# Rearranged start of an attention-and-MLP kernel: first chunk on hardware queues, weight folded by blocks, filler matmuls, one transpose moved to PE

## Chip, cores, metric

One core of a Trainium2 chip. The metric is the device time of one execution in microseconds (us), as the median of several; "span" is the time from the first to the last instruction in a trace. The wait that a view gives for PE runs from the modelled end of the matmul before; from start to start about 0.16 us more of PE's time is lost.

## The reference

```python
# q, k, v: (4, 6080, 256) float32; moe_w_in (256, 2048); moe_w_out (2048, 256)
qn = q / (norm(q, axis=1) + 1e-6);  kn = k / (norm(k, axis=1) + 1e-6)   # norms over the 6080 rows
s  = kn.transpose(0, 2, 1) @ qn / tau                # 256 x 256 for each of 4 batches
a  = softmax(s)                                      # last axis
x  = (v @ a).reshape(24320, 256)
h  = relu(x @ w_in)
out = (moe_s * h * h + moe_b) @ w_out
```

## The kernel before

For each batch the kernel sums the 256 x 256 Gram matrix of k and q and the squares for the norms, takes the exponentials, and folds the attention matrix into the first weight (`wa` = a @ w_in), so that v goes straight through `wa`. A fold is two matmuls and an eviction, which copies their result out of PSUM, where the kernel lets matmuls write (for 128x512 of it 0.69 us on ACT, 0.75 on DVE). The main loop is 48 groups of 512 rows of v, in 16 steps each: a step is `mm1` (two matmuls of 512 columns into `h_ps`), a relu on ACT, a square on DVE, and `mm2` of the steps four and five earlier (four matmuls of 256 into `o_ps`). Everything else (Gram matmuls of the next batch, loads, casts) is hung on steps with `at_step`.

```python
        def load(self, c):                       # all chunks: POOL queue, cast fp32 -> fp16 in flight
            at, np_, jc = self.chunks[c]
            ...
            for t, src in ((kc, k), (qc, q)):
                po(nc.gpsimd.dma_start(out=t[:np_, :jc, :], in_=...))
    ...
    for c in range(len(g0.chunks)):
        g0.load(c)
    po(nc.gpsimd.dma_start(out=w_in16, in_=...))            # whole first weight, then v
    load_v(0)
    for h in range(2):
        po(nc.gpsimd.dma_start(out=w_out32[...], in_=...))  # second weight, two halves
    load_v(1); load_v(2)
    ...
    nc.sync.dma_start(out=s_bc, in_=moe_s.to_broadcast((P, 1)))   # 128 reads of 4 bytes
    nc.sync.dma_start(out=b_bc, in_=moe_b.to_broadcast((P, 1)))
    ...
    for f in fin[:3]: f()           # norms, reciprocals, transposes of S
    transpose_v(0)                  # first group of v: on PE
    for f in fin[3:]: f()           # exponentials, sums, all eight folds of 512 columns
    ...
        if g >= 1:                  # every later group of v: transposed by DMA (crossbar)
            at_step(max((g - 2) * FT, 4 * (g - 1)) + 6, lambda g=g: crossbar_v(g))
    ...
    def fold_w(fo, m):              # 2 matmuls, then an eviction: m == 0 on ACT, m == 1 on DVE
    ...
    def rowconst_sum(i, n): ...     # 8 sums on DVE, one a step from step 8
    at_step(8 + len(todo), rowconst_mm)
```

## Time and profile before

| | before |
|---|---|
| time, median of 4 | 769.46 us (769.11 to 769.82) |
| span | 768.4 us |
| PE busy | 734.9 us, 96% |
| first h_ps matmul (start of the main loop) | 48.91 us |
| PE idle, waiting for group 1 (the second; counted from 0) | 5.0 us before 65.99, then half clock to 71.6 |

The lines of the profile are in the prediction below. A window row gives the busy time of PE, PEld (weight loads), DVE, ACT and POOL, then the granted PE clock, the DMA engines' busy share and GB/s written. A timeline row is start, length, engine, source line, operation, and in brackets the idle time before it and what is thought to have ended it.

### The profile page before, as it was taken

To read this page: it belongs to the slowest core of one execution; us is meant where nothing else is said; L and a number is where in the kernel's file an instruction comes from. 1 tells how busy PE (TensorE), PEld (TensorE's weight loads), DVE (VectorE), ACT (ScalarE), POOL (GpSimd) and SP (SyncE) were. 2 spreads that over 40 slices of the span, in tenths; PEclk is the share of its full clock that TensorE was granted. 3 is DMA by queue.
4 is the path that set the end of the run, shared out by engine and by line. 5 is a ranking of instruction groups with operands and counts; after the bars stand their busy time and mean duration, and the time that the engine had idled before them with its cause. 6 is when DMAs were issued, how large, how long until landed. Compare 5 with 4: busy or idle time off the path is not lost.

```text
span 768.4 us, 14012 instructions
## 1 busy us (share of the span) xinstructions
PE 734.9 (96%) x5274; PEld 507.1 (66%) x5274; DVE 479.4 (62%) x1059; ACT 517.7 (67%) x858; POOL 57.3 (7%) x111
## 2 busy tenths in 40 slices
PE   3587999999999999999999999999999999999997
PEld 2444666666667666666667666666667766666666
DVE  3755666766566666667556666676656556565565
ACT  3464777776767777667777667777676666666665
POOL 3411010001000100000001001000000000000000
PEclk9888999999999999999999999999999999999999
DMA  8999945325555274235626565324322333212111
GB/s 155 212 263 173 159 100 112 82 67 115 123 127 132 62 150 108 67 70 109 145 63 121 113 145 114 70 69 80 72 57 77 76 69 90 65 46 83 42 64 42
DMA packets 75988, 78.52 MB, mean 102 GB/s; under 512 B 56320, under 2 KB 56896, under 8 KB 75920
## 3 DMA queue, kind: packets, MB, share of 16 engines
q0 software_dynamic: 15152, 40.51, 28.5%
q1 hardware_dynamic: 60768, 37.12, 18.1%
q8 instruction: 41, 0.67, 0.4%
q14 instruction: 27, 0.22, 0.1%
HBM read 78.91 MB, written 24.90 MB: 135 GB/s over the span
## 4 chain that ended last, share of the span: by engine, by line
PE 90%; DMA 7%; issue 1%; ACT 1%; SPq 0%; POOL 0%; DVE 0%; POOLq 0%
PE o_ps L450 42%; PE h_ps L426 42%; PE s_ps L120 4%; DMA qc<-in_q_dram 4%; DMA v<-in_v_dram 2%; DMA vT<-v 2%; PE wa_ps L237 1%; SPq L283 0%; PE n_ps L185 0%; ACT r L429 0%; ACT eT L214 0%; PE t_ps L208 0%; POOL kc L108 0%; POOL w_out L295 0%; PE rc_ps L347 0%
## 5 line engine op out<-in xcount | busy, mean ns | idle before, releaser
L429 ACT ACTIVATE r<-h_ps 128x512 f16<-128x512 f32 (+1 forms) x768 | 449.9, 593 | 211.9 <-PE h_ps L426 185.0
L436 DVE TENSOR_TENSOR g<-r 128x512 f16<-128x512 f16 (+1 forms) x768 | 320.7, 421 | 254.9 <-ACT r L429 248.0
L426 PE MATMUL h_ps<-vT,wa 128*128 128x512 f16 (+7 forms) x1632 | 454.4, 365 | 5.6 <-DMA vT<-v 5.0
L450 PE MATMUL o_ps<-w_out,g 128*128 128x256 f16 x3040 | 458.3, 273 | 0.0
L450 PEld LDWEIGHTS <-g 128*128 128x128 f16 x3040 | 295.8, 98 | 184.6 <-issue 2.2
L426 PEld LDWEIGHTS <-wa 128*128 128x128 f16 x1632 | 159.6, 98 | 36.2 <-issue 6.3
L120 PE MATMUL s_ps<-qc,kc 128*128 128x256 f16 (+1 forms) x384 | 71.8, 291 | 19.3 <-DMA qc<-in_q_dram 19.2
L458 DVE SCALAR_TENSOR_TENSOR o_sb<-o_ps,s_out,rowconst 128x512 f32<-128x512 f32 x95 | 71.1, 749 | 6.5 <-PE o_ps L450 5.7
L261 POOL DMA_DIRECT2D v<-in_v_dram x48 | 25.8, 537 | 585.2 <-DMA vT<-v 452.7
L143 ACT ACTIVATE sq<-kc 128x1024 f16<-128x1024 f16 (+3 forms) x49 | 50.0, 1031 | 22.0 <-DMA kc<-in_k_dram 18.8
L120 PEld LDWEIGHTS <-kc 128*128 128x128 f16 (+1 forms) x384 | 39.9, 104 | 27.3 <-issue 10.9
L140 DVE TENSOR_TENSOR sq<-qc 128x1024 f16<-128x1024 f16 (+3 forms) x49 | 32.6, 676 | 11.5 <-DMA qc<-in_q_dram 11.5
L156 DVE TENSOR_TENSOR f<-sq 128x1024 f16<-128x1024 f16 (+1 forms) x47 | 31.8, 686 | 0.3
L156 DVE TENSOR_TENSOR f<-f 128x512 f16<-128x512 f16 (+3 forms) x47 | 25.9, 551 | 0.4
L237 PE MATMUL wa_ps<-w_in,eT 128*128 128x512 f16 x64 | 19.8, 415 | 0.0
L242 ACT ACTIVATE wa<-wa_ps,rs 128x512 f16<-128x512 f32 x16 | 11.0, 687 | 9.3 <-PE wa_ps L237 5.2
L108 POOL DMA_DIRECT2D kc<-in_k_dram x26 | 14.2, 546 | 16.0 <-DMA kc<-in_k_dram 8.9
L108 POOL DMA_DIRECT2D qc<-in_q_dram x26 | 14.2, 547 | 9.6 <-DMA qc<-in_q_dram 8.0
L244 DVE TENSOR_SCALAR wa<-wa_ps,rs 128x512 f16<-128x512 f32 x16 | 11.9, 746 | 2.3 <-PE wa_ps L237 2.1
L237 PEld LDWEIGHTS <-eT 128*128 128x128 f16 x64 | 6.6, 105 | 3.7 <-issue 2.5
L214 ACT ACT_TABLE_LOAD x4 | 5.1, 1283 | 0.5 <-DVE rnrm L196 0.5
L343 DVE TENSOR_TENSOR w_out<-w_out 128x512 f32<-128x512 f32 (+1 forms) x8 | 5.2, 651 | 0.0
(37 smaller groups left out, 41.8 us busy)
## 6 DMA issues: line engine op xcount, KB each, us to landing
out_dram<-o_sb SPq DMA_DIRECT2D x47, 512.0 KB, 2.9
v<-in_v_dram POOLq DMA_DIRECT2D x47, 256.0 KB, 3.8
kc<-in_k_dram POOLq DMA_DIRECT2D x20, 512.0 KB, 6.0
qc<-in_q_dram POOLq DMA_DIRECT2D x20, 512.0 KB, 8.8
vT<-v SPq DMA_TRANSPOSE x186, 2.4
w_out<-in_moe_w_out_dram POOLq DMA_DIRECT2D x2, 1024.0 KB, 13.6
kc<-in_k_dram POOLq DMA_DIRECT2D x3, 480.0 KB, 5.7
qc<-in_q_dram POOLq DMA_DIRECT2D x3, 480.0 KB, 8.3
```

Source lines behind the costliest of these rows:

```text
L108: po(nc.gpsimd.dma_start(out=t[:np_, :jc, :], in_=src[self.b, at : at + np_ * jc, :].rearrange("(p j) c -> p j c", j=jc)))
L120: po(nc.tensor.matmul(self.s_ps[:, ch, :], kc[:np_, j, ts(ch, P)], qc[:np_, j, :], start=(c == 0 and j == 0 and ch == 0), stop=(c == len(s ...
L140: po(nc.vector.tensor_mul(st["sq"][:np_, 0, js, :], qc[:np_, js, :], qc[:np_, js, :]))
L143: po(nc.scalar.activation(out=st["sq"][:np_, 1, js, :], in_=kc[:np_, js, :], func=AF.Square))
L156: po(nc.vector.tensor_add(st["f", half][:np_, arrays], src[:np_, arrays, :half, :], src[:np_, arrays, half : 2 * half, :]))
L237: po(nc.tensor.matmul(wa_ps, st["e"][:, j, ts(m, P)], w_in16[:, j, ds(fo * NW, NW)], start=(j == 0), stop=(j == CH - 1)))
L261: po(nc.gpsimd.dma_start(out=v16[:, :nj, :], in_=v_flat[t0 : t0 + nj * P, :].rearrange("(p j) c -> p j c", j=nj)))
L426: po(nc.tensor.matmul(dst, wa[:, ci, ts(m, P)], src, start=(ci == 0), stop=(ci == CH - 1), skip_group_check=True))
L429: po(nc.scalar.activation(out=r16[:, :n], in_=h_ps[:, :n], func=AF.Relu))
L436: po(nc.vector.tensor_mul(g16[:, :n], r16[:, :n], r16[:, :n]))
L450: po(nc.tensor.matmul(o_halves[g, h][:, j % 2, :], g16[:, ts(j, P)], w_out16[:, m, :], start=(m == 0 and j == js[0]), stop=(m == FT - 1 an ...
L458: po(nc.vector.scalar_tensor_tensor(out=o_sb[:, js[0] : js[-1] + 1, :], in0=o_halves.pop((g, h)), scalar=s_out, op0=ALU.mult, in1=rowconst ...
```

## The change

Intent: bring the main loop forward and take the hole behind the first group out. The first chunk comes uncast on the two hardware queues (those of SP and ACT) and is cast on DVE and ACT; POOL makes the identities before its first load; the broadcasts of s and b go behind the third v on the POOL queue; most norm sums stand ahead of the last chunk; a quarter of the first weight comes before v, two 256-wide blocks of it are folded before the loop and the other six folds in it; eight filler matmuls stand in PE's gaps; group 1 of v is transposed on PE at step 12.

```diff
+            direct = self.b == 0 and c == 0
...
+                if direct:
+                    raw = w_out32[:, ds(i * JC, JC), :]
+                    (nc.sync, nc.scalar)[i].dma_start(out=raw, in_=rows)
...
+        def cast(self, c):
...
+                po(nc.vector.tensor_copy(out=kc[:, js, :], in_=w_out32[:, js, :]))
+                po(nc.scalar.copy(out=qc[:, js, :],
+                                  in_=w_out32[:, JC + js.start : JC + js.stop, :]))
...
-    nc.sync.dma_start(out=s_bc, in_=moe_s.to_broadcast((P, 1)))
...
+    load_w_in(0, NW)
+    load_v(0)
+    load_w_in(NW, Dff)
...
+    load_v(2)
+    s_bc = consts.tile([P, 1], FP32)
+    po(nc.gpsimd.dma_start(out=s_bc, in_=moe_s.to_broadcast((P, 1))))
...
+        if c == NCH0 - 1:
+            g0.add_norms()
...
+    fin[0]()
+    fin[1]()
+    keep_busy(6)
+    fin[2]()
     transpose_v(0)
-    for f in fin[3:]:
+    keep_busy(2)
+    for f in fin[3:9]:
...
-    for i in range(1, 8):
-        at_step(i - 1, lambda i=i: cast_w_out(i))
+    for i, f in enumerate(fin[9:]):
+        at_step(i // 2 * 4 + i % 2 + 1, f)
...
+    for i in range(8):
+        at_step(i + 2, lambda i=i: cast_w_out(i))
...
-            at_step(max((g - 2) * FT, 4 * (g - 1)) + 6, lambda g=g: crossbar_v(g))
+            if g == 1:
+                at_step(12, lambda g=g: transpose_v(g))
+            else:
+                at_step((g - 2) * FT + 6, lambda g=g: crossbar_v(g))
```

More of the change, by code (lines that the diff above doesn't have):

```diff
@@ L100, in __init__ @@
             self.tiles = {}
-            self.rows = []
+            self.rows, self.n_ps = [], None
         def load(self, c):
@@ L106, in load @@
             qc = qk_pool.tile([P, JC, C], FP16, tag="qc", name="qc")
-            for t, src in ((kc, k), (qc, q)):
-                po(nc.gpsimd.dma_start(
-                    out=t[:np_, :jc, :],
-                    in_=src[self.b, at : at + np_ * jc, :].rearrange("(p j) c -> p j c", j=jc)))
-            self.tiles[c] = qc, kc
+            direct = self.b == 0 and c == 0
+            for i, (t, src) in enumerate(((kc, k), (qc, q))):
+                rows = src[self.b, at : at + np_ * jc, :].rearrange("(p j) c -> p j c", j=jc)
+                if direct:
+                    raw = w_out32[:, ds(i * JC, JC), :]
+                    (nc.sync, nc.scalar)[i].dma_start(out=raw, in_=rows)
+                else:
+                    po(nc.gpsimd.dma_start(out=t[:np_, :jc, :], in_=rows))
+            self.tiles[c] = qc, kc
+        def cast(self, c):
+            qc, kc = self.tiles[c]
+            for h in range(2):
+                js = slice(h * JC // 2, (h + 1) * JC // 2)
+                po(nc.vector.tensor_copy(out=kc[:, js, :], in_=w_out32[:, js, :]))
+                po(nc.scalar.copy(out=qc[:, js, :],
+                                  in_=w_out32[:, JC + js.start : JC + js.stop, :]))
         def start(self):
@@ L174, in norm_ops, with add_norms @@
             return ops + [fold(2, slice(0, 2), False), fold(1, slice(0, 2), True)]
+        def add_norms(self, last=False):
+            first = self.n_ps is None
+            if first:
+                self.n_ps = ps_h.tile([P, 2, CH], FP32, tag="h_ps", name="n_ps")
+            todo = [(t, np_, j, a, ch) for t, np_, jc in self.rows for j in range(jc)
+                    for a in range(2) for ch in range(CH)]
+            self.rows = []
+            for i, (t, np_, j, a, ch) in enumerate(todo):
+                po(nc.tensor.matmul(self.n_ps[:, a, ch : ch + 1], t[:np_, a, j, ts(ch, P)],
+                                    ones16[:np_, 0:1], start=(first and i == 0),
+                                    stop=(last and i == len(todo) - 1), skip_group_check=True))
         def finish_ops(self):
@@ L180, in norms @@
             def norms():
-                n_ps = ps_h.tile([P, 2, CH], FP32, tag="h_ps", name="n_ps")
-                todo = [(t, np_, j, a, ch) for t, np_, jc in self.rows for j in range(jc)
-                        for a in range(2) for ch in range(CH)]
-                for i, (t, np_, j, a, ch) in enumerate(todo):
-                    po(nc.tensor.matmul(n_ps[:, a, ch : ch + 1], t[:np_, a, j, ts(ch, P)],
-                                        ones16[:np_, 0:1], start=(i == 0),
-                                        stop=(i == len(todo) - 1), skip_group_check=True))
+                self.add_norms(last=True)
                 nrm = sm_pool.tile([P, 2, CH], FP32, tag="nrm", name="nrm")
-                po(nc.scalar.activation(out=nrm, in_=n_ps, func=AF.Sqrt))
+                po(nc.scalar.activation(out=nrm, in_=self.n_ps, func=AF.Sqrt))
                 st["nrm"] = nrm
@@ L229, in sums, with fold_w @@
                 po(nc.vector.reciprocal(out=st["rs"], in_=st["rs"]))
-            NW = 512
-            def fold_w(fo, m):
+            def fold_w(f0, n, m):
                 def f():
@@ L236, in f @@
                     for j in range(CH):
-                        po(nc.tensor.matmul(wa_ps, st["e"][:, j, ts(m, P)],
-                                            w_in16[:, j, ds(fo * NW, NW)],
+                        po(nc.tensor.matmul(wa_ps[:, :n], st["e"][:, j, ts(m, P)],
+                                            w_in16[:, j, ds(f0, n)],
                                             start=(j == 0), stop=(j == CH - 1)))
-                    dst = self.wa[:, m, ds(fo * NW, NW)]
+                    dst = self.wa[:, m, ds(f0, n)]
                     if m == 0:
-                        po(nc.scalar.mul(out=dst, in_=wa_ps, mul=st["rs"][:, m : m + 1]))
+                        po(nc.scalar.mul(out=dst, in_=wa_ps[:, :n], mul=st["rs"][:, m : m + 1]))
                     else:
                         po(nc.vector.tensor_scalar_mul(
-                            out=dst, in0=wa_ps, scalar1=st["rs"][:, m : m + 1]))
+                            out=dst, in0=wa_ps[:, :n], scalar1=st["rs"][:, m : m + 1]))
                 return f
-            return [norms, recip, turn, exps, sums] + [
-                fold_w(fo, m) for fo in range(Dff // NW) for m in range(CH)]
+            widths = ([NW // 2] * 2 if self.b == 0 else [NW]) + [NW] * (Dff // NW - 1)
+            folds, f0 = [], 0
+            for n in widths:
+                folds += [fold_w(f0, n, m) for m in range(CH)]
+                f0 += n
+            return [norms, recip, turn, exps, sums] + folds
     def group(g):
@@ L284, in crossbar_v @@
         vT_tiles[g] = vT
-    grams = {b: Gram(b, chunks_first if b == 0 else chunks_later) for b in range(B)}
-    g0 = grams[0]
-    for c in range(len(g0.chunks)):
-        g0.load(c)
-    po(nc.gpsimd.dma_start(out=w_in16, in_=moe_w_in.rearrange("(co p) f -> p co f", p=P)))
-    load_v(0)
-    w_out_rows = moe_w_out.rearrange("(fo p) d -> p fo d", p=P)
-    for h in range(2):
-        po(nc.gpsimd.dma_start(out=w_out32[:, ts(h, FT // 2), :], in_=w_out_rows[:, ts(h, FT // 2), :]))
-    load_v(1)
-    load_v(2)
     ident16 = consts.tile([P, P], FP16)
@@ L305, with load_w_in @@
     nc.vector.memset(ones32, 1.0)
-    s_bc = consts.tile([P, 1], FP32)
-    nc.sync.dma_start(out=s_bc, in_=moe_s.to_broadcast((P, 1)))
-    b_bc = consts.tile([P, 1], FP32)
-    nc.sync.dma_start(out=b_bc, in_=moe_b.to_broadcast((P, 1)))
-    s_out = consts.tile([P, 1], FP32)
-    nc.vector.tensor_scalar_mul(out=s_out, in0=s_bc, scalar1=1.0 / (LAM * LAM))
+    grams = {b: Gram(b, chunks_first if b == 0 else chunks_later) for b in range(B)}
+    g0 = grams[0]
+    assert FT == 2 * JC
+    g0.load(0)
     warm = consts.tile([P, 1], FP32)
     po(nc.scalar.activation(out=warm, in_=ones32[:, 0:1], func=AF.Sqrt))
+    g0.cast(0)
+    for c in range(1, len(g0.chunks)):
+        g0.load(c)
+    NW = 512
+    w_in_rows = moe_w_in.rearrange("(co p) f -> p co f", p=P)
+    def load_w_in(f0, f1):
+        po(nc.gpsimd.dma_start(out=w_in16[:, :, f0:f1], in_=w_in_rows[:, :, f0:f1]))
+    load_w_in(0, NW)
+    load_v(0)
+    load_w_in(NW, Dff)
+    w_out_rows = moe_w_out.rearrange("(fo p) d -> p fo d", p=P)
+    for h in range(2):
+        po(nc.gpsimd.dma_start(out=w_out32[:, ts(h, FT // 2), :], in_=w_out_rows[:, ts(h, FT // 2), :]))
+    load_v(1)
+    load_v(2)
+    s_bc = consts.tile([P, 1], FP32)
+    po(nc.gpsimd.dma_start(out=s_bc, in_=moe_s.to_broadcast((P, 1))))
+    b_bc = consts.tile([P, 1], FP32)
+    po(nc.gpsimd.dma_start(out=b_bc, in_=moe_b.to_broadcast((P, 1))))
+    s_out = consts.tile([P, 1], FP32)
     g0.start()
-    for c in range(len(g0.chunks)):
+    NCH0 = len(g0.chunks)
+    for c in range(NCH0):
         ops = g0.norm_ops(c)
+        if c == NCH0 - 1:
+            g0.add_norms()
         for j in range(g0.chunks[c][2]):
@@ L322, with keep_busy @@
             f()
+    def keep_busy(n):
+        idle_ps = ps_h.tile([P, TG], FP32, tag="h_ps", name="idle_ps")
+        for _ in range(n):
+            po(nc.tensor.matmul(idle_ps, w_in16[:, 0, :P], w_in16[:, 0, :NW],
+                                start=True, stop=True, skip_group_check=True))
     fin = g0.finish_ops()
-    for f in fin[:3]:
-        f()
+    fin[0]()
+    fin[1]()
+    keep_busy(6)
+    fin[2]()
     transpose_v(0)
-    for f in fin[3:]:
+    keep_busy(2)
+    for f in fin[3:9]:
         f()
@@ L335, in cast_w_out @@
             po(nc.vector.tensor_copy(out=w_out16[:, part, :], in_=w_out32[:, part, :]))
-    cast_w_out(0)
     def rowconst_sum(i, n):
@@ L356 @@
     first_group = [b * N // TG for b in range(B)]
-    for i in range(1, 8):
-        at_step(i - 1, lambda i=i: cast_w_out(i))
+    for i, f in enumerate(fin[9:]):
+        at_step(i // 2 * 4 + i % 2 + 1, f)
+    at_step(14, lambda: po(nc.vector.tensor_scalar_mul(
+        out=s_out, in0=s_bc, scalar1=1.0 / (LAM * LAM))))
+    for i in range(8):
+        at_step(i + 2, lambda i=i: cast_w_out(i))
     todo = [(i, n) for n in (FT * C // 2, FT * C // 4, FT * C // 8, FT * C // 16)
@@ L367 @@
         if g >= 1:
-            at_step(max((g - 2) * FT, 4 * (g - 1)) + 6, lambda g=g: crossbar_v(g))
+            if g == 1:
+                at_step(12, lambda g=g: transpose_v(g))
+            else:
+                at_step((g - 2) * FT + 6, lambda g=g: crossbar_v(g))
     for b in range(1, B):
```

## The prediction

> **What bounds the kernel now.** I read the page first (busy shares, slices), then the windows of the first 72 us, then PE's timeline there, and last the chain, the waits and the DMA issues.
>
> The slices of the page:
>
> ```profile
> span 768.4 us, 14012 instructions
> ...
> PE   3587999999999999999999999999999999999997
> ...
> PEclk9888999999999999999999999999999999999999
> DMA  8999945325555274235626565324322333212111
> ```
>
> A slice is 19.2 us. From the fifth slice on PE is busy without a gap: the main loop is PE-bound to the end, and nothing in the diff makes its matmuls cheaper. All that can be won lies in the first four slices. The windows of that stretch (columns: window, its length, busy time of PE, PEld, DVE, ACT and POOL, PE clock, DMA share, GB/s):
>
> ```profile
> 2.00:4.00 2.00, 0.00 (x0) 0.00 (x0) 0.15 (x1) 0.22 (x2) 2.00 (x5) 1.00 0.58 39
> 4.00:6.00 2.00, 0.00 (x0) 0.00 (x0) 0.00 (x0) 0.00 (x0) 1.62 (x4) 1.00 1.02 158
> 6.00:8.00 2.00, 0.00 (x0) 0.00 (x0) 0.00 (x0) 0.00 (x0) 0.00 (x0) 1.00 0.72 99
> 8.00:10.00 2.00, 0.00 (x0) 0.10 (x1) 0.00 (x0) 1.77 (x2) 0.54 (x1) 1.00 1.04 209
> ...
> 41.00:47.00 6.00, 4.44 (x21) 2.21 (x22) 1.67 (x4) 1.37 (x2) 1.59 (x3) 0.50 1.04 375
> ...
> 61.00:66.00 5.00, 0.01 (x1) 0.04 (x2) 2.46 (x6) 0.20 (x1) 0.00 (x0) 0.85 1.33 156
> 66.00:71.60 5.60, 5.60 (x20) 3.06 (x21) 1.34 (x3) 1.49 (x3) 3.18 (x6) 0.52 0.80 144
> ```
>
> To be seen: the DMA engines do not reach their steady 209 GB/s before 8 us; PE runs its first fold at half clock (0.50 from 41 to 47 us); PE stands from 61 to 66 us and pays for it with half clock (0.52) until 71.6. PE's timeline gives the borders (start, length):
>
> ```profile
> 36.85 0.68 PE L185 MATMUL n_ps<-ones,sq 128*128 128x1 f16 x16 [0.18 <-DVE sq L140]
> 39.10 0.63 PE L208 MATMUL t_ps<-ident,sm_s 128*128 128x128 f32 x4 [1.57 <-DVE sm_s L201]
> 42.56 1.04 PE L272 MATMUL vT_ps<-ident,v 128*128 128x128 f16 x8 [2.83 <-DMA v<-in_v_dram]
> 43.55 5.53 PE L237 MATMUL wa_ps<-w_in,eT 128*128 128x512 f16 x16
> ...
> 65.99 1.01 PE L426 MATMUL h_ps<-vT,wa 128*128 128x512 f16 x2 [4.99 <-DMA vT<-v]
> ```
>
> So the main loop starts behind a wait for v (2.83 us) and 5.53 us of cold fold; the first h_ps matmul comes at 48.91 us in this timeline. The chain of waits names the later stall, the waits what else hangs on it, and the DMA issues how long a transfer queues (last figure: median us from issue to landing):
>
> ```profile
> 52.78 13.07 DMA vT<-v
> ```
>
> ```profile
> POOL v L261 <- DMA vT<-v: 16.5, 1, 16.5
> PE h_ps L426 <- DMA vT<-v: 5.0, 1, 5.0
> ```
>
> ```profile
> w_in<-in_moe_w_in_dram POOLq DMA_DIRECT2D x1, 1024.0 KB, 12.9
> ...
> vT<-v SPq DMA_TRANSPOSE x12, 10.1
> ...
> qc<-in_q_dram POOLq DMA_DIRECT2D x1, 96.0 KB, 9.2
> ```
>
> With the issue times of the POOL timeline (26.22 for the last q, 28.42 for w_in, 30.94 with 11.6 to landing for the first v, 32.19 and 33.39 with 12.9 and 14.3 for w_out), the landings are: last q 35.4, w_in 41.3, v 42.5, w_out 45.1 and 47.7 us. One 512 KB chunk, cast from 1 MB, takes 2.43 us in steady state (the chunks' consumers start at 15.88, 20.85, 25.71, 30.68, two chunks apart).
>
> [...] a DMA share over 1.0 with one queue carrying 88% of it. The hardware queue can therefore win the slow start, not a faster stream. [...] from 52.5 to 62.5 us the crossbar's 256-byte packets go out about one per cast packet, some 50 to 60 per us, and over 300 in half a us once the POOL queue is empty at 63 us. [...] 0.50 after the hole from 37.5 to 42.6, recovery some 5 us after the restart at 66.
>
> **The change part by part.** Times are of the clock of before, shifted as I go.
>
> 1. *First chunk on the hardware queues, s and b moved back.* q and k of the first batch are 12.45 MB of fp32: 12.45/1.05 x 2.43 = 28.8 us of streaming. Landing at 35.4[...] the stream behaves as if begun at 6.0 us. In the trace the first POOL packets start at 2.6 us and then crawl beside the 4-byte packets of the two broadcasts until 7.5 us. The hardware queues gave a first packet at 2.0 us (the broadcast of s), and the broadcasts go behind the third v. A full stream from about 3.7 us gives 2.3 us; the ceiling, from 3.0, is 2.9. The identities now stand ahead of POOL's first load (1.2 us of POOL work), hidden behind 2 MB on the hardware queues. Casts: on DVE two of 128x1024; by the 0.42 us of 128x512 and the slope of such a cast, 0.69 each, 1.4 us. On ACT 1.04 each (as its 1024-wide squares), 2.1 us. DVE has 3.7 us of work per 4.86 us pair of chunks, so it catches up by the fourth pair. Gain 2.3.
>
> 2. *Early norm sums.* They leave 8 matmuls at the end for the 40 of before. But DVE, not PE, is last there: its last square of q ends at 37.1 and n_ps at 37.53. In program order the last chunk's four matmuls now stand behind the sixth chunk's norms, which wait for a DVE square at 36.7. I take a loss of 0.3.
>
> 3. *First quarter of w_in, then v.* The quarter costs 1.2 us of transfer for the 4.9 of the whole, so v lands 3.7 earlier: 42.5 - 3.7 - 2.3 = 36.5, before the transposes of S are done. After n_ps (37.53 - 2.3 + 0.3 = 35.5) come 1.57 of root, reciprocal and product, with six fillers in them (6 x 0.216 = 1.3 warm; 2.6 cold would delay by 1.0), 0.63 of transposes, 0.7 of v's transposes with two fillers (0.43), all beside the Exp table load (1.28) and two exponentials (0.84); then sums (0.3), rs (0.5 with its wait), a 256-wide eviction (0.5). First h_ps at 35.5 + 1.6 + 0.6 + 0.7 + 0.4 + 0.3 + 0.6 + 0.5 = 40.2, say 40.3: 8.6 us before 48.91. This holds gain 1, the wait for v and the cold fold.
>
> 4. *The other six folds go into the loop.* 12 matmuls of 512 at 0.216 = 2.6 us, on PE, which is the bound: given back. Their evictions and the w_out casts fit: in steps 0 to 10 ACT has about 9.7 us of work against PE's 10.4.
>
> 5. *w_out.* Its first half lands at 45.1 - 2.3 = 42.8, cast by 43.3; PE wants it at step 4, 40.3 + 5 x 0.43 + 2 x 0.43 = 43.3. Just met; with ACT's pile-up in steps 0 to 4 I put 0.6 for small stalls.
>
> 6. *Group 1 on PE.* Removes the 5.1 us hole (60.85 to 65.99) and the half clock after it: 5.6 us at 0.52 lose 2.7. Adds eight transposes at about 0.09[...], 0.7.
>
> Sum: 8.6 - 2.6 - 0.6 + 7.8 - 0.7 = 12.5 us. 769.7 - 12.5 = 757.2, 1.6%.
>
> **The rivals.**
> (a) *The stall moves to group 2.* Its crossbar transposes still fight the POOL queue, and POOL no longer stands 16.5 us behind group 1's crossbar: one more v and a k/q pair come in (1.2 + 4.9 us), so the queue empties at 63 - 2.3 + 6.1 = 66.8 and the transposes land near 68. PE needs them at step 32: 40.3 + 15.5 (sixteen steps with folds and transposes) + 13.9 + 2 (Gram matmuls and the row constant) = 71.7. Four us of slack; if it is eaten, 2 to 5 us plus half clock come back: 760 to 764. I give it 12%.
> (b) *The slow start is the memory waking up, not the broadcasts or the software queue.* Then part 1 gives under 1 us: 758.5. [...] against it: the slow stretch is just where the 4-byte packets are.
> (c) *PE stays cold.* If fillers come late for w_in or run cold, about 1 us at the turn and up to 2 in the folds: 760.
> (d) *Everything adds up to more than 2%.* That needs 15.4 us. With the ceiling of part 1 and no stalls I reach 13.7, so something unseen would be needed.
>
> **Range and chances.** 757.0 us; 8 times in 10 between 754.6 and 760.8: below by the ceiling of part 1 and of the stalls, above by one rival of 1 to 4 us. Faster by over 2% (under 754.3): 0.09. Within 2%: 0.90. Slower: 0.01.
>
> **What would show it.** Right: last q's landing near 33 us; DMA at over 350 GB/s (uncast bytes) before 8 us; the first h_ps near 40.3 us; PE clock 1.00 from 36 us on; no idle PE over 1 us after that; no wait for vT; from 90 us on, the same loop, shifted by about 12.5 us. Wrong: a PE wait for vT at group 2, a wait of o_ps for the w_out cast, a clock of 0.5 anywhere after 36 us, or DMA still at 100 to 160 GB/s from 4 to 8 us. If all steps hold and the time is still off by over 3 us, the loop behind 90 us changed, which I don't expect.

From the kernel before: a DMA share of 1.04 at 209 GB/s (8 to 10 us), with 87.8% of the 16 engines' time for the POOL queue from 0 to 90 us; 592 packets of the POOL queue and 576 of the crossbar from 52.5 to 62.5 us; and PE's clock at 0.50 from 40.6 to 47.4 and from 64.5 to 71.3 us. The sum came to 12.5 us, but the 2.3 us of part 1, which stand in its 8.6, start from 6.0 us, and 35.4 - 28.8 is 6.6: the rest is latency. That the first chunk has to be cast on chip is an assumption which no run tests; the 0.09 is the estimate (eight transposes took 0.45 us in the changed kernel).

## The result

The changed kernel took 760.21 us (759.92 to 760.68, 4 runs) against 769.46: a ratio of 0.988 (95% interval 0.9863 to 0.9898), 9.2 us or 1.2% faster, inside 2%. A ratio is the mean time of one kernel's fast runs over that of the other's of the same rounds, so not quite the ratio of the medians quoted. All runs were fast ones (granted clock 0.995 to 0.998). The profiled span fell by 10.3 us.

The page of the changed kernel:

```profile
span 758.1 us, 14053 instructions
...
PE   2689999999999999999999999999999999999998
...
PEclk9999999999999999999999999999999999999999
DMA  9999963337356553326546376233323234312111
```

PE is full from the fourth slice of 19 us on, where it took until the fifth before, and no slice is below 0.9 of full clock. The windows of the changed kernel's start, set against those of before:

```profile
2.00:4.00 2.00, 0.00 (x0) 0.00 (x0) 0.00 (x0) 0.65 (x2) 2.00 (x5) 1.00 0.76 262
4.00:6.00 2.00, 0.00 (x0) 0.00 (x0) 0.00 (x0) 0.00 (x0) 1.99 (x4) 1.00 1.04 418
6.00:8.00 2.00, 0.00 (x0) 0.00 (x0) 0.00 (x0) 0.00 (x0) 0.00 (x0) 1.00 1.01 346
...
41.00:47.00 6.00, 5.01 (x29) 2.54 (x27) 3.78 (x9) 5.08 (x11) 1.20 (x3) 1.00 0.92 257
47.00:61.00 14.00, 11.98 (x82) 7.43 (x80) 11.63 (x26) 8.51 (x15) 1.46 (x3) 1.00 0.96 173
61.00:66.00 5.00, 5.00 (x37) 3.53 (x36) 3.44 (x7) 3.48 (x7) 0.00 (x0) 1.00 0.97 174
```

The stream is at full rate at 4 us (418 GB/s at a DMA share of 1.04, since the first chunk is not halved by a cast; the cast stream of before wrote 209 at the same share), the clock stays at 1.00 from 30 us to the end of the loop (before that it was 0.83 from 20 to 30 us), and the hole from 61 to 66 us is gone. But PE is not full between 41 and 61 us: 16.99 us busy out of 20. PE's timeline shows where:

```profile
39.78 1.04 PE L476 MATMUL h_ps<-vT,wa 128*128 128x512 f16 x4
...
43.75 0.39 PE L476 MATMUL h_ps<-vT,wa 128*128 128x512 f16 x1 [0.99 <-DVE wa L262]
...
48.66 0.39 PE L476 MATMUL h_ps<-vT,wa 128*128 128x512 f16 x1 [0.52 <-DVE wa L262]
...
53.70 0.39 PE L476 MATMUL h_ps<-vT,wa 128*128 128x512 f16 x1 [0.52 <-DVE wa L262]
...
59.41 0.67 PE L390 MATMUL rc_ps<-w_out,ones 128*128 128x256 f32 x2 [0.97 <-PE o_ps L500]
```

The loop starts at 39.78 us, and then stands four times, for 0.99, 0.52, 0.52 and 0.97 us: 3.0 us in all. For the first three the DVE timeline and that of ACT show the queue in front of the folded weight:

```profile
42.60 0.43 DVE L486 TENSOR_TENSOR g<-r 128x512 f16<-128x512 f16 x1 [0.64 <-ACT r L479]
42.95 0.75 DVE L262 TENSOR_SCALAR wa<-wa_ps,rs 128x512 f16<-128x512 f32 x1
...
58.90 0.41 DVE L386 TENSOR_TENSOR w_out<-w_out 128x256 f32<-128x256 f32 x1
```

```profile
41.40 0.69 ACT L260 ACTIVATE wa<-wa_ps,rs 128x512 f16<-128x512 f32 x1
41.97 1.21 ACT L479 ACTIVATE r<-h_ps 128x512 f16<-128x512 f32 x2
```

The eviction of the second half of a fold (42.95) stands in DVE's order behind the square of its step (42.60), that square waits for the relu of its step, and the relu stands on ACT behind the eviction of the first half (41.40). PE needs the columns two steps after the fold and asks too early. DVE does not overtake here: it idles 0.64 us before the square at 42.60 us, though the fold whose eviction stands behind that square ended at 41.52 + 0.59 = 42.11 us. The fourth wait is put down to o_ps, but DVE's last sum for the row constant ends at 58.90 + 0.41 = 59.31, right before rc_ps at 59.41.

### The profile page after: what moved, and what is told of

Read it like the earlier page. It is cut to its first block, busy times and chain, and to the rows that moved or that the text cites. A ratio compares the mean times of both kernels' runs of the same rounds, so it can differ in the third digit from the quotient of the medians.

```text
span 758.1 us, 14053 instructions
## 1 busy us (share of the span) xinstructions
PE 730.5 (96%) x5294; PEld 505.3 (67%) x5294; DVE 480.9 (63%) x1063; ACT 520.1 (69%) x861; POOL 57.8 (8%) x112
## 4 chain that ended last, share of the span: by engine, by line
PE 92%; DMA 3%; DVE 2%; ACT 1%; issue 1%; POOL 1%; DVEq 0%; ACTq 0%; POOLq 0%
PE o_ps L500 43%; PE h_ps L476 42%; PE s_ps L133 4%; DMA qc<-in_q_dram 3%; PE wa_ps L255 1%; ACT r L479 1%; DVE f L169 0%; DVE g L486 0%; ACT eT L234 0%; PE n_ps L198 0%; DVE sq L153 0%; POOL kc L114 0%; DVE wa L262 0%; PE t_ps L228 0%; POOL qc L114 0%
## 5 line engine op out<-in xcount | busy, mean ns | idle before, releaser
L133 PE MATMUL s_ps<-qc,kc 128*128 128x256 f16 (+1 forms) x384 | 69.4, 283 | 18.9 <-ACT qc L123 10.8
L156 ACT ACTIVATE sq<-kc 128x1024 f16<-128x1024 f16 (+3 forms) x49 | 49.9, 1031 | 10.4 <-DMA kc<-in_k_dram 7.4
L255 PE MATMUL wa_ps<-w_in,eT 128*128 128x512 f16 (+1 forms) x68 | 18.9, 366 | 0.0
L260 ACT ACTIVATE wa<-wa_ps,rs 128x512 f16<-128x512 f32 (+1 forms) x17 | 11.2, 662 | 4.6 <-PE wa_ps L255 4.6
L262 DVE TENSOR_SCALAR wa<-wa_ps,rs 128x512 f16<-128x512 f32 (+1 forms) x17 | 12.1, 714 | 0.1
L123 ACT CAST qc<-w_out 128x1024 f16<-128x1024 f32 x2 | 2.0, 1042 | 7.0 <-DMA w_out<-in_q_dram 7.0
```

The lines of the kernel that those rows point to most:

```text
L133: po(nc.tensor.matmul(self.s_ps[:, ch, :], kc[:np_, j, ts(ch, P)], qc[:np_, j, :], start=(c == 0 and j == 0 and ch == 0), stop=(c == len(s ...
L156: po(nc.scalar.activation(out=st["sq"][:np_, 1, js, :], in_=kc[:np_, js, :], func=AF.Square))
L255: po(nc.tensor.matmul(wa_ps[:, :n], st["e"][:, j, ts(m, P)], w_in16[:, j, ds(f0, n)], start=(j == 0), stop=(j == CH - 1)))
```

## The experiments

"Span" is that of all runs of a kernel; the changed kernel's own were 757.9 to 758.2. Different calls ran on different chips or at other times: the kernel before had spans of 767.1 to 768.9 in them, so differences under half a us between calls say little. b_sb_tiny and a_norms_end have two runs, b_sb_late one, whose state is unknown; all others have four, and all of these are fast.

| run | what | median us | ratio to before | spans |
|---|---|---|---|---|
| (changed kernel) | | 760.21 | 0.988 | 757.9 to 758.2 |
| b_g1_pe | before + group 1 on PE | 764.13 | 0.9936 | 762.3 to 763.5 |
| a_g1_crossbar | changed, group 1 on crossbar | 771.29 | 1.0016 | 769.0 to 770.1 |
| a_w_in_whole | changed, weight whole | 763.36 | 0.9924 | 760.8 to 761.8 |
| a_no_fill | changed, no fillers | 761.30 | 0.989 | 759.4 to 760.1 |
| a_sw_chunk | changed, chunk on POOL queue | 761.54 | 0.9899 | 759.0 to 759.4 |
| a_norms_end | changed, norm sums at the end | 759.64 | 0.9876 | 757.8 to 758.0 |
| b_sb_late | before + broadcasts late | 771.53 (1 run) | - | 769.8 |
| b_sb_tiny | before + no broadcasts | 766.86 | 0.997 | 765.1 |
| e_folds_early | changed, folds a step earlier | 758.64 | 0.9854 | 756.7 to 757.1 |
| e_both | and row constant two steps later | 757.66 | 0.984 | 755.4 to 756.1 |
| e_sb_tiny | and no broadcasts | 758.54 | 0.9863 | 756.5 to 756.8 |
| e_order | and weights in order of use | 758.55 | 0.9863 | 756.1 to 756.6 |

All gave correct results.

### The waits in the loop: e_folds_early, e_both

```diff
-        at_step(i // 2 * 4 + i % 2 + 1, f)
+        at_step(i // 2 * 4 + i % 2, f)
```

> The changed kernel with the six folds of the loop each one step earlier. My theory: PE's three waits for a DVE eviction of the folded weight (0.99, 0.52 and 0.52 us in the changed kernel) come from the fold being handed to ACT and DVE, which work in order, only two steps before its columns are used; one step (0.43 to 0.87 us) more takes them away: span 758.1 less 1.8 to 2.0 = 756.1 to 756.3, and no wait of h_ps for wa. Rival: ACT or the w_out casts are short in steps 0 to 6, then the waits only change place and the span stays within 0.4 of 758.1. The wait before rc_ps (0.97) stays under both.

Measured: 756.7 to 757.1, 1.3 us less. The second and third wait are gone, the first shrank from 0.99 to 0.50, a new one of 0.27 for the cast of the second weight stands beside it, and the row constant waits 1.22 instead of 0.97. So the theory holds for its mechanism, and I had its first wait wrong: in steps 0 to 4 ACT and the second weight are short too, as the rival said.

```diff
-    at_step(8 + len(todo), rowconst_mm)
+    at_step(10 + len(todo), rowconst_mm)
```

> The folds one step earlier and the matmul of the row constant two steps later. My theory: the hole of 0.97 us before rc_ps is a wait for DVE's last row-constant sum, which ends at 59.3 us, and two steps (1.7 us) later it is done: all four holes gone, 758.1 less 3.0 = 755.1, in time about 757.2. Rival: the hole is a wait for a free PSUM buffer or the sums only slip further back, then no better than the folds alone (756.2).

Measured: 755.4 to 756.1, 2.3 us under the changed kernel by the means (755.8 and 758.1), not 3.0. PE's waits in e_both (total, times, longest) after the loop's start:

```profile
PE h_ps L476 <- DVE wa L262: 0.4, 1, 0.4
PE o_ps L500 <- DVE w_out L380: 0.3, 1, 0.3
```

The wait at rc_ps is gone, so it was DVE's sums; in e_folds_early, too, the last of them ends at 57.94 and rc_ps starts at 58.03. Behind it a Gram matmul now waits 0.47 us for the first q chunk of the second batch, which the hole had covered. This version, with two numbers changed, beats both kernels: 757.66 us, ratio 0.984.

### Group 1: a_g1_crossbar, b_g1_pe

```diff
-            if g == 1:
-                at_step(12, lambda g=g: transpose_v(g))
-            else:
-                at_step((g - 2) * FT + 6, lambda g=g: crossbar_v(g))
+            at_step(max((g - 2) * FT, 4 * (g - 1)) + 6, lambda g=g: crossbar_v(g))
```

> The changed kernel with the second group of v turned by the crossbar again, as in the kernel before. My theory: its transposes start at about 50 us and land only once the POOL queue has run dry at 62 to 65 us, while PE asks for them near 58: a hole of 4 to 7 us, and half clock for some 5 us after it (2.5 lost), less 0.45 of transposes on PE and less the 3.0 us of small stalls if DVE catches up in the hole (at most 1.0 of them, the one at rc_ps): 758.1 + 5 to 9 = 763 to 767. Rival: the other parts have freed the DMA queues by then, the transposes land in time, and the span is 757.6 to 758.5.

Measured: 769.0 to 770.1, outside what I expected and 11.4 us over the changed kernel: with group 1 on the crossbar all the rest of the change gains nothing. Its waits and its chain:

```profile
PE h_ps L473 <- DMA vT<-v: 10.5, 1, 10.5
```

```profile
51.98 15.39 DMA vT<-v
```

PE asks at 57 us and gets group 1 at 67.4, later than the 65.9 of before: the landing does not follow PE. The DMA engines move 196 to 200 GB/s all through the hole (58 to 66 us), and from 58 to 64 us 373 packets of the POOL queue and 373 of the crossbar go out. The landing follows the POOL queue's running dry. In the four traces with group 1 on the crossbar (before, this run, b_sb_late, b_sb_tiny) the transposes are first issued at 48.9, 46.5, 46.9 and 46.8 us, the POOL queue's last packet goes at 64.4, 66.4, 66.2 and 62.4, and group 1 lands at 65.9, 67.4, 67.5 and 63.3. An earlier loop only lengthens the hole.

The opposite edit in the kernel before:

> The kernel before with one part alone: the second group of v turned on PE at step 12. Theory one (the crossbar hole is worth itself): hole of 5.1 us and 2.7 of half clock gone, 0.5 to 0.8 of transposes added: span 768.4 less 7.0 to 7.4 = 761.0 to 761.4. Theory two (after the run that put group 1 back on the crossbar in the changed kernel and fell to 770.1): the crossbar's landing sets the time whatever stands before it, so this part alone is most of the whole gain; same number, but then the rest of the change is worth only the difference to 758.1, about 3 us. A span above 764 would say that another wait takes the hole's place.

Measured: 762.3 to 763.5, or by the ratio 4.9 us of gain, less than the 7.0 to 7.4 I expected. The hole is gone, but a smaller one opened where it had been:

```profile
PE rc_ps L347 <- issue: 1.5, 1, 1.5
```

This is the row constant again: the last of its sums on DVE ends at 63.02, rc_ps starts at 63.13. They were late in the kernel before too, and the crossbar's hole had covered them. So the part alone brings 4.9, the others alone (a_g1_crossbar) nothing or a loss of 1, and all together 9.2: the others, with which the POOL queue ran dry no earlier (66.4 against 64.4 us), pay only once group 1 is off the crossbar.

### The start of the stream: b_sb_late, b_sb_tiny, a_sw_chunk

b_sb_late: in the kernel before, the two broadcasts moved to the POOL queue behind the third v.

> The kernel before with only the two 4-byte broadcasts moved from the front of the hardware queue to the POOL queue behind the third v; the first chunk stays on the software queue. My theory from the prediction: the broadcasts' packets halve the stream from 5 to 7.5 us, so the first q lands at 9.0 to 9.5 instead of 11.0 us, the last q at 33.2 to 34 instead of 35.4, and the span falls by 1.5 to 2.2, to 766.2 to 766.9. Rival: it is the memory or the software queue waking up: first q at 10.7 to 11.1, last q near 35, span within 0.5 of 768.4.

Measured, in one run: the first Gram matmul at 9.07 us instead of 11.04 and the main loop at 46.27 instead of 48.91, so the broadcasts were the slow start, as predicted (up to 1 us of the 2.6 at the loop is chance, see below); but the span rose to 769.8. Two windows of this run:

```profile
4.00:6.00 2.00, 0.00 (x0) 0.00 (x0) 0.00 (x0) 0.00 (x0) 1.61 (x4) 1.00 1.07 211
...
48.00:50.00 2.00, 2.00 (x14) 1.19 (x13) 1.10 (x3) 2.00 (x5) 0.73 (x1) 1.00 0.43 74
```

From 4 to 6 us the stream runs at 211 GB/s where it had 158, but from 48 to 50 us, where the broadcasts now are, at 74. The cost was moved, not removed, the POOL queue ran dry later, and group 1's crossbar with it (PE waited 9.3 us). The expectation missed this because it looked at one end only.

b_sb_tiny: one element of each is loaded, and a matmul with a row of ones spreads them at step 14.

```diff
-    s_bc = consts.tile([P, 1], FP32)
-    nc.sync.dma_start(out=s_bc, in_=moe_s.to_broadcast((P, 1)))
...
+    nc.sync.dma_start(out=sb_row[:, 0:1], in_=moe_s.to_broadcast((1, 1)))
+    nc.sync.dma_start(out=sb_row[:, 1:2], in_=moe_b.to_broadcast((1, 1)))
...
+        po(nc.tensor.matmul(sb_ps, ones32[0:1, :], sb_row, start=True, stop=True))
+        po(nc.vector.tensor_copy(out=sb_bc, in_=sb_ps))
```

> The kernel before with s and b loaded as single elements and spread by a small matmul, nothing else. If the broadcasts cost about 2 to 3 us of DMA time wherever they stand, then without any the first q lands at 9.0 to 9.3, the POOL queue runs dry 2 us earlier than at 63, the crossbar's transposes land near 63.8 and the span is 766.0 to 766.8 (with the broadcasts merely moved back it was 769.8). Rival: the crossbar's landing does not follow the POOL queue, and the span is 768 or more.

Measured: first Gram matmul at 8.93, 215 GB/s from 45 to 50 us, span 765.1, even better than expected: 2.1 to 2.7 us under most runs of the kernel before on the same chip (767.2 to 767.8; one was 768.6). The hole for group 1 is still 5.1 us long, but everything ends earlier.

a_sw_chunk: in the changed kernel, `direct = False` and no cast on chip.

> The changed kernel with its first chunk back on the software queue, cast in flight, and no casts on chip; the broadcasts stay late. If the broadcasts were the slow start, only the later start of the POOL queue is lost (about 1 us, as it now stands behind the identities): span 758.1 + 0.3 to 1.2. If the hardware queue itself is the gain: last q about 2.2 us later than the 33.2 of the changed kernel and span about 760.3.

Measured: 759.0 to 759.4, 1.1 us over the changed kernel; the first h_ps at 40.43 instead of 39.78. So of the 2.2 us by which the last q came earlier, the hardware queues and casts account for about 0.65 us by the loop's start, where POOL makes the identities first, and the broadcasts' removal from the front for the rest.

### The first weight, the fillers, the norm sums: a_w_in_whole, a_no_fill, a_norms_end

a_w_in_whole: `load_w_in(0, Dff)` ahead of v, and `for f in fin[3:]` before the loop.

> The changed kernel with w_in in one load before v and all eight folds before the loop, no split of the first. By the sum: v lands near 40.3 instead of about 36.5, the fillers wait for w_in until about 39, the first h_ps comes near 45 instead of 39.8 (5.2 later), but the loop is rid of 2.6 us of folds and of its 2.0 us of waits on evictions: span 758.1 + 0.3 to 1.0. Rival: the split load is where the gain of the start comes from, 2.5 us or more lost: 760.6 and above.

Measured: 760.8 to 761.8, 3.4 us over the changed kernel: the rival was right. The fillers stand 2.7 us for the whole weight, the clock falls (0.50 from 40 to 42 us), and the first h_ps comes at 46.33, not 45; the half clock is what my sum had left out.

a_no_fill: both `keep_busy` calls removed.

> The changed kernel without the eight filler matmuls. Theory one: the gaps they fill (1.57 us before the transposes of S, 0.4 before the sums) are shorter than what drops PE's clock, so nothing happens: span 758.1 within 0.4, clock 1.00 at 36 to 45 us. Theory two: the clock falls to 0.5 as it did in the kernel before at 41 us, and the folds and first steps cost 1.5 to 3 us more: 759.6 to 761.

Measured: 759.4 to 760.1, 1.5 us over the changed kernel. The window and the folds of this run:

```profile
39.00:40.00 1.00, 0.91 (x9) 0.48 (x8) 0.90 (x3) 0.05 (x1) 0.00 (x0) 0.50 1.04 403
```

```profile
37.32 0.85 PE L228 MATMUL t_ps<-ident,sm_s 128*128 128x128 f32 x4 [1.57 <-DVE sm_s L221]
...
39.21 1.98 PE L255 MATMUL wa_ps<-w_in,eT 128*128 128x256 f16 x8
```

The clock is 0.50 from 38 to 41 us and the eight folds take 1.98 us; with the fillers they take 1.03. One gap of 1.57 us, with thin work around it, was enough to lose the clock. (Of the 1.5 us, 0.35 were there before the gap: the last norm sum ends at 35.75, in the changed kernel at 35.40.) Theory two holds, at the low end of its size.

a_norms_end: the call of `add_norms` before the last chunk removed, so that `norms` does all of them at the end.

> The changed kernel with all norm sums at the end of the first batch again. DVE's last squares are what is waited for, 32 small matmuls more behind them: my prediction said a loss of 0.3 from doing them early, the trace of the changed kernel showed 0.1. Span within 0.4 of 758.1, if anything lower; the intent of the change would say 0.8 to 1.2 higher, as 32 matmuls of about 26 ns join the chain.

Measured: 757.8 to 758.0. The early norm sums gain nothing: PE does 24 of the 40 while DVE is at its last squares, and its last norm sum ends 0.41 us after them (35.24 and 34.83), against 0.71 in the changed kernel (35.40 and 34.69).

### What was left: e_sb_tiny, e_order

Built on e_both. e_sb_tiny has the edit of b_sb_tiny.

> The mended kernel (folds a step earlier, row constant two steps later, span 756.1) with s and b loaded as one element each and spread over the partitions by a small matmul at step 14, in place of the two 128-way 4-byte broadcasts on the POOL queue. My theory: the broadcasts throttle the DMA engines from 45 to 50 us (117 to 134 GB/s there); without them the first q chunk of the second batch is in time and PE's 0.47 us wait for it goes: span 755.4 to 755.8, DMA over 180 GB/s from 45 to 50 us. Rival: the dip is the POOL queue waiting for buffers, not the broadcasts: DMA stays under 140 there and the span at 756.

Measured: a miss. The mechanism is there, by the window of this run:

```profile
45.00:50.00 5.00, 5.00 (x35) 3.23 (x34) 3.36 (x9) 4.54 (x9) 1.06 (x2) 1.00 1.11 212
```

The DMA is at 212 GB/s and PE's wait for q is gone; its last output is issued at 753.03 us, against 753.19 in e_both. Yet the span is 756.7, because the end of the program after that issue took 3.7 us instead of 2.9. The cause of that tail is open; the run shows only that it lies after the last output and not on PE. It need not be this edit's: over all kept traces the tail is 2.9 to 3.75 us, and 3.75 in b_sb_late, which has the broadcasts.

e_order: besides, the second quarter of w_in and the first of w_out before the rest, and both folds of the first block at step 0.

> The same, and besides the weights in the order of use (second quarter of w_in, first quarter of w_out, the rest of each) and both folds of the loop's first block at step 0. Theory: the two small waits left in steps 4 and 5 (0.45 for the folded weight, 0.28 for the w_out cast) go: 0.5 to 0.7 under the run before it, about 754.9. Rival: ACT is full there (relu, eviction and cast one after another from 40 to 45 us), the waits only move: within 0.2 of the run before.

Measured: 756.1 to 756.6, as e_sb_tiny within 0.3. The two waits became one of 0.68 us for the second weight's cast: the rival was right, they only moved.

## Why the prediction was right, and where its size was off

The range held; the middle, 757.0, was 3.2 us low. That the time still fell into the range is partly luck: the room above the middle was kept for rivals (a) to (c), none of them came, and what filled it was term 5. By its own steps:

1. **Start of the stream (2.3 us).** Right: the last q landed at 24.00 + 9.2 = 33.2 us, 2.2 earlier. Also right that the broadcasts held the stream up (b_sb_late). Two inputs were loose: 2.43 us a chunk is one of three intervals, whose mean is 2.47, and the start at 6.0 us holds a latency that no view shows (the last packet of q starts at 35.0 us, 0.4 before its landing at 35.4). Not seen: that the broadcasts cost about as much at their new place (DMA at 110 GB/s from 44 to 49 us in the changed kernel). That costs PE nothing there, since the row constant's wait covers it, and 0.47 us in e_both.
2. **Early norms (0.3 lost).** Right in the trace (0.71 against 0.41 us in a_norms_end); in the span the difference of 0.2 is within the noise.
3. **Start of the loop (40.3 us).** 39.78, half a us better. The fillers were needed (1.5 us), and the split of the weight (3.4 us). About 1 us of the 9.1 gained here is chance: in b_g1_pe, which starts as the kernel before does, the clock was at half from 38.6 to 45.4 us, not from 40.6 to 47.4, and the loop began at 47.88, not 48.91.
4. **Folds given back (2.6 us).** As predicted, by the length of the twelve matmuls.
5. **Small stalls (0.6 us).** This is the term that failed. It was 3.0 us by the waits shown, and 3.65 counted as the prediction counted the hole, from where the next matmul would have started (1.15, 0.68, 0.68 and 1.14). The prediction compared the sums of work on ACT and PE over ten steps (9.7 against 10.4 us) and from that took the folds to fit; but what PE waits for is one eviction at a given step, and that stood two steps behind its fold, behind other work in the order of two engines (the 0.64 us for which DVE idles before the square at 42.60 us). e_folds_early and e_both took 2.3 us of it back with nothing but places in the order. The 0.97 of them at the row constant was a wait hidden under the crossbar's hole in the kernel before; b_g1_pe, where the hole is taken away alone, shows it as 1.5. The w_out cast, which the prediction had in this term, was no wait in the changed kernel, and appeared at 0.27 once the folds were earlier.
6. **Group 1 (7.8 less 0.7).** Hole 5.15 us by the same count, and from the first h_ps of group 1 to the first Gram matmul 5.65 us before and 4.25 - 1.14 = 3.11 after, so 2.5 of half clock: 7.7 in all. The transposes took 0.45 for the 0.7 of the sum. Rival (a) did not come: no PE wait for vT is left. It read the POOL queue as empty at 63 us (its last packet goes at 64.4), but group 2 was there by 67.05, when POOL's wait for its buffer ends, and PE asks for it at 74.26.

With the measured terms the sum is 9.1 - 2.6 - 3.65 + 7.7 - 0.45 = 10.1 us, and the first Gram matmul of the loop, which has all of this behind it, comes 10.0 us earlier (61.66 for 71.64). The span fell by 10.3, since the end of the program after the last output is issued took 2.9 us for 3.2. The time fell by 9.2 only. 0.5 of that difference is the choice of the runs that were profiled: the one of the kernel before took 770.23 us, more than all four of the comparison. 0.6 is the part of the time outside the span, 2.4 us in the profiled run of the changed kernel and 1.8 in the other. It was 2.4 to 2.8 us in two of the four runs of the changed kernel, and 1.7 to 1.8 in the other two and in the runs of the kernel before that list both. Why is open. So of the 3.2 us that were missing, 3.0 are term 5; the terms that came out better (0.65) and what lies outside the terms (0.8) nearly cancel.

What the prediction did not say, and the runs show: the terms were added as if independent, and they are not. Terms 1 to 3 are worth nothing while group 1 waits for a landing that the POOL queue sets (a_g1_crossbar).

## What to carry to other kernels

When work is moved into a loop that PE bounds, check not only that each engine has the time, but for each moved piece in which step its result is needed and what stands before it in the order of the engine that delivers it; leave a step more than seems needed. A large hole covers smaller ones, so before counting its whole length as gain, look for late work beside it. And a gain ahead of a wait that another queue ends is no gain until that wait is taken away, or that queue ends earlier (b_sb_tiny).

## What else the traces show of the clock and the DMA queues

- One gap of 1.57 us was enough to lose PE's clock here. In a_no_fill the clock fell at 37.6 us, after a gap from 35.75 to 37.32 with mostly one-column matmuls in the 1.6 us before it, and was back at 41.0; with eight fillers it stayed at 1.00. In b_sb_tiny it fell at 36.4 us, 0.7 us after PE's last matmul, with 1.5 us of one-column matmuls before that. How long a gap it takes no run here settles.
- Two 128-way broadcasts of 4 bytes cost the stream about 2 us when at the front of the hardware queue (first Gram matmul at 11.04 us, against 8.93 without them), and on the POOL queue held it to 69 to 74 GB/s for 4 us (b_sb_late), against 211 to 220 without (b_sb_tiny).
- A DMA transpose beside a cast stream took 11.4 us in the median (4.6 to 14.1) from issue to landing for the eight of the start of the kernel before, 2.4 us in the median over the whole kernel.
